# The last layer's second product for two token chunks, in seven block products instead of eight

## The chip, the cores and the metric

One core of one Trainium2 chip runs the whole program. The metric is the device time of one execution in microseconds (us); the kernel before took 581.81 us (median of 3 runs, 581.29 to 582.12).

## The reference

Attention (2 batches, 8 heads, 768 positions, 64 features a head; a local window of 16 and one pooled key and value for each block of 32) gives a matrix `x` of 1536 tokens by 512 features. Two feed-forward layers follow, each with weights 512 x 2048 and 2048 x 512, all in fp32:

```
h = x @ w_in;  r = max(h, 0);       x = (s * r * r + b) @ w_out      # layer 0
h = x @ w_in;  g = max(0.01*h, h);  out = g @ w_out                  # layer 1
```

The change touches layer 1 alone: `g @ w_out`, and how `out` lies in memory.

## The kernel before

Tokens go in three chunks of 512 (chunks 1, 2, 3; the code counts from 0), the hidden 2048 features in 16 slices `fc` of 128. To keep fp32 accuracy each operand is split into a rounded "high" part and a "low" rest, and each 128 x 128 by 128 x 512 product is three matmuls: high by high, low by high, high by low. ScalarE (ACT) makes the high part by a copy (`split_hi` L427, `split_block` L657, `ffn_hi` L470), VectorE (DVE) or GpSimd (POOL) the low part by a subtraction (`split_lo` L433, L658, `ffn_lo` L479).

Chunk 1 of layer 1 runs slice by slice: 12 matmuls of the first product (`ffn_in` L442), the activation, 12 of the second (`ffn_out` L494). For chunks 2 and 3 the first product is already done in Winograd's form of Strassen's scheme: the 512 x 512 blocks of hidden features by tokens come in eight quads `j`, each of four blocks, from seven block products in place of eight (`block` L668; 6 matmuls each; a11, s2, a12, s3, a22, s1, s4 name the weight block or the sum of blocks that is multiplied). Every block product has its own PSUM bank, and VectorE adds the results up (`after_block` L693 to L712). Beside these blocks run the second products of chunk 2 (units of 3 matmuls, taken from a list `queue`); chunk 3's second product comes last, alone (`last_chunk`): 16 slices of 12 matmuls. Each unit accumulates 128 tokens by 512 features in one of four banks; `out_store` copies the banks to SBUF and sends them to `out`, 1536 x 512. The last tile is sent in two halves, from the ACT queue and from the SP queue (L525, L526).

The order on every engine is the order in which the program issues instructions (`manual_schedule`); engines take their own instructions in that order, and semaphores are set from the tiles that are read and written.

Of the kernel before, what the change touches and what calls it, by code (L numbers as in the profile page):

```python
# [10 lines left out]
F32 = mybir.dt.float32  # L11
F32R = mybir.dt.float32r
# [20 lines left out]
GU = 4  # L33
# [66 lines left out]
def block_attention_moe_moe(ctx, tc, q, k, v, vn, w1, w2, mask, ident_in, pool_in, out):  # L100
# [380 lines left out]
    def ffn_out(i, m):  # L481
        layer, c, fc = steps[i]
        w, g = ws[1][i], gs[i]
        acc = accs.setdefault((layer, c), {})
        if fc == 0 and m not in acc:
            acc[m] = ps_acc.tile([P, 512], F32, name="acc")
        ms = slice(m * P, (m + 1) * P)
        for a, b in ((0, 0), (1, 0), (0, 1)):
            first = fc == 0 and a == 0 and b == 0
            last = fc == NFC - 1 and b == 1  # L490
            if layer == 0:
                nc.tensor.matmul(acc[m], lhsT=w[:, a, ms], rhs=g[:, b, :], start=first, stop=last)  # L492
            else:
                nc.tensor.matmul(acc[m], lhsT=g[:, b, ms], rhs=w[:, a, :], start=first, stop=last)  # L494

    xf = {1: {}, 2: {}}

# [16 lines left out]
        )  # L514

    def out_store(c, m):
        acc = accs[1, c]
        o = kpool_.tile([P, 1024], F32, name="kt")[:, :DM]
        t0 = c * 512 + m * P
        if c == 2 and m == 3:  # L520
            for cols, copy, queue in (
                (slice(0, DM // 2), nc.scalar.copy, nc.scalar),
                (slice(DM // 2, DM), nc.vector.tensor_copy, nc.sync),
            ):
                copy(o[:, cols], acc[m][:, cols])  # L525
                queue.dma_start(out[t0 : t0 + P, cols], o[:, cols])  # L526
            return
        if m % 2:
            nc.scalar.copy(o, acc[m])
        else:  # L530
            nc.vector.tensor_copy(o, acc[m])
        nc.sync.dma_start(out[t0 : t0 + P, :], o)


    NQ, LEAD = NFC // 2, 3
# [219 lines left out]
    def last_chunk():  # L755
        for fc in range(NFC):
            i = ns - NFC + fc
            if fc == 0:
                accs[1, 2] = {m: bank() for m in range(4)}
                late_split(1, 0)  # L760
            if fc + 1 < NFC:
                late_split(1, fc + 1)
            if fc == 0:
                for m in range(4):
                    out_store(1, m)
            for m in range(4):
                ffn_out(i, m)
        for m in range(4):
            out_store(2, m)
# [175 lines left out]
    for i in range(n_ffn1, nq):  # L945
        if i + 1 < nq:
            first_in(i + 1)
        else:
            block(1, 0, 0)
            block(1, 0, 1)  # L950
        if i + 2 < nq:
            split_hi(i + 2, 0)
            split_lo(i + 2, 0, nc.gpsimd)
        elif i + 2 == nq:
            for n in range(LEAD):
                split_block(1, n)
        if i + 1 < nq:
            split_hi(i + 1, 1)
            split_lo(i + 1, 1, nc.vector)
        if i + 1 < nq:  # L960
            chain(i + 1)
        at = i - n_ffn1
        convert((at + 1) * left // 13 - at * left // 13)
        if i + 1 < nq:
            for m in range(4):
                ffn_out(i, m)
        at -= 1
        if 0 <= at < 10:
            token_forms(at // 5, at % 5)
        if at == 11:  # L970
            weight_forms(1, 0)

    queue += [("out", nq - 1, m) for m in range(4)] + [("store", 0)]
    quads(1, 0, 2)
    emit_out(len(queue))
    last_chunk()


_INS = ["q", "k", "v", "vn", "w1", "w2", "mask", "ident", "pool"]
# [69 lines left out]
```

## Time and profile before

| | before |
|---|---|
| median of 3 runs | 581.81 us |
| profiled execution, span from first to last instruction | 579.6 us |
| TensorE matmul busy | 565.9 us, 98%, 3171 matmuls |
| DVE, ACT, POOL busy | 392.0, 341.1, 249.1 us |
| granted TensorE clock | full in all of the 40 slices |

The page shows one profiled execution. Its span is 2.2 us under the median of the runs; the page gives no other time for it. "PE" are matmuls, "PEld" weight loads, "L494" line 494.

### The profile page before, as it was taken

How to read it: one execution, taken by the hardware profiler on the slowest of the kernel's cores; microseconds unless marked ns; L12 is line 12 of the kernel's file. 1: busy time of each engine (PE TensorE's matmuls, PEld its weight loads, DVE VectorE, ACT ScalarE, POOL GpSimd, SP SyncE). 2: the span in 40 equal slices, each digit the busy share in tenths (PEclk: the TensorE clock that was granted, in tenths of full speed). 3: DMA queues.
4: the chain of work that ended last, by engine and by line, in shares of the span. 5: the costliest groups of instructions: out<-in, count | busy, mean ns of one | idle time of the engine just before them, and what ended most of it. 6: DMA issues, size and time to landing. Idle time of an engine off the chain costs nothing.

```text
span 579.6 us, 8972 instructions
## 1 busy us (share of the span) xinstructions
PE 565.9 (98%) x3171; PEld 454.9 (78%) x3172; DVE 392.0 (68%) x773; ACT 341.1 (59%) x770; POOL 249.1 (43%) x298
## 2 busy tenths in 40 slices
PE   3999999999999999999999999999999999999997
PEld 3567788777778888888888888888888888887885
DVE  5889987665689866665666889997354444446543
ACT  3888768776666555445656666764455444545442
POOL 4444644442262555524451436556565555540000
PEclk9999999999999999999999999999999999999999
DMA  8967765572100000000242345551010000000101
GB/s 324 399 219 246 250 205 211 174 233 95 74 2 1 1 1 1 1 1 1 73 131 88 110 126 165 145 146 36 1 72 2 1 1 0 1 0 12 62 2 72
DMA packets 16436, 53.38 MB, mean 92 GB/s; under 512 B 2024, under 2 KB 2664, under 8 KB 15752
## 3 DMA queue, kind: packets, MB, share of 16 engines
q1 hardware_dynamic: 16104, 52.69, 27.3%
q8 instruction: 25, 0.41, 0.3%
q14 instruction: 19, 0.16, 0.1%
q10 hardware_dynamic: 288, 0.13, 0.1%
HBM read 49.08 MB, written 3.15 MB: 90 GB/s over the span
## 4 chain that ended last, share of the span: by engine, by line
PE 96%; DMA 3%; SPq 0%; DVE 0%; issue 0%; ACT 0%
PE acc L492 23%; PE h L442 22%; PE acc L494 15%; PE h L668 10%; PE at L668 10%; PE h L494 4%; PE at L494 4%; DMA kt<-in_k 2%; PE at L334 2%; PE at L254 2%; PE at L353 2%; DMA w<-in_q 1%; PE h L353 1%; PE acc L442 0%; PE at L220 0%; PE at L208 0%
## 5 line engine op out<-in xcount | busy, mean ns | idle before, releaser
L492 PE MATMUL acc<-g,wout 128*128 128x512 f32 x564 | 141.6, 393 | 0.0
L442 PE MATMUL h<-xt,win 128*128 128x512 f32 x564 | 138.5, 392 | 0.0
L442 PEld LDWEIGHTS h<-xt,win 128*128 128x128 f32 x564 | 104.8, 188 | 22.7 <-issue 1.1
L492 PEld LDWEIGHTS acc<-g,wout 128*128 128x128 f32 x564 | 104.5, 188 | 22.6 <-issue 0.9
L494 PE MATMUL acc<-wout,g 128*128 128x512 f32 x384 | 99.1, 391 | 0.0
L433 DVE TENSOR_TENSOR wout<-w,wout 128x512 fp32r<-128x512 f32 x82 | 64.1, 782 | 37.6 <-ACT wout L427 37.2
L427 ACT CAST wout<-w 128x512 fp32r<-128x512 f32 x95 | 58.8, 619 | 46.7 <-PE acc L492 22.7
L494 PEld LDWEIGHTS acc<-wout,g 128*128 128x128 f32 x384 | 72.0, 188 | 15.8 <-DVE wout L433 0.4
L433 POOL TENSOR_TENSOR win<-w,win 128x512 fp32r<-128x512 f32 x36 | 52.0, 1444 | 51.4 <-ACT win L427 37.9
L413 DVE SCALAR_TENSOR_TENSOR w<-st,w 128x512 int32<-128x512 int32 x64 | 59.0, 925 | 6.8 <-issue 3.2
L658 POOL TENSOR_TENSOR win<-q,win 128x256 fp32r<-128x256 f32 x48 | 39.4, 820 | 37.8 <-ACT win L657 37.1
L658 POOL TENSOR_TENSOR win<-w,win 128x256 fp32r<-128x256 f32 x36 | 30.0, 833 | 44.2 <-ACT win L657 31.8
L479 DVE TENSOR_TENSOR g<-r,g 128x512 fp32r<-128x512 f32 x32 | 23.0, 719 | 36.4 <-ACT g L470 36.3
L393 ACT ACTIVATE st<-st 128x512 f32<-128x512 f32 x64 | 41.3, 673 | 0.7 <-DMA st<-in_w 0.7
L427 ACT CAST win<-w 128x512 fp32r<-128x512 f32 x48 | 29.5, 615 | 13.5 <-PE h L442 7.5
L668 PE MATMUL h<-xt,win 128*128 128x512 f32 x132 | 33.8, 391 | 0.0
L668 PE MATMUL at<-xt,win 128*128 128x512 f32 x132 | 33.8, 391 | 0.0
L680 ACT ACTIVATE r<-r 128x512 f32<-128x512 f32 x16 | 10.1, 632 | 37.9 <-DVE r L679 37.9
L475 DVE SCALAR_TENSOR_TENSOR g<-h,own,g 128x512 fp32r<-128x512 f32 x31 | 23.2, 748 | 12.8 <-ACT g L468 12.8
L406 POOL TENSOR_SCALAR w<-st 128x512 int32<-128x512 uint8 x30 | 23.5, 784 | 17.3 <-DMA st<-in_w 12.8
L668 PEld LDWEIGHTS h<-xt,win 128*128 128x128 f32 x132 | 24.8, 188 | 5.5
L668 PEld LDWEIGHTS at<-xt,win 128*128 128x128 f32 x132 | 24.8, 188 | 5.5
(185 smaller groups left out, 924.7 us busy)
## 6 DMA issues: line engine op xcount, KB each, us to landing
st<-in_w SPq DMA_DIRECT2D x64, 512.0 KB, 3.6
vt<-in_v SPq DMA_DIRECT2D x5, 1024.0 KB
kt<-in_k SPq DMA_DIRECT2D x8, 500.0 KB, 5.8
out<-kt SPq DMA_DIRECT2D x11, 256.0 KB, 2.7
q<-in_q SPq DMA_DIRECT2D x8, 256.0 KB, 4.6
w<-in_vn SPq DMA_DIRECT2D x3, 512.0 KB, 10.1
w<-in_q SPq DMA_DIRECT2D x4, 256.0 KB, 11.7
w<-in_v SPq DMA_DIRECT2D x2, 512.0 KB
```

The lines of the kernel that those rows point to most:

```text
L393: nc.scalar.activation(out=high, in_=high, func=AF.Prelu, scale=2.0**-112, alpha=2.0**32)
L406: engine.tensor_scalar(f, byte, 1.0 / 32, -31.0 / 64, op0=ALU.mult, op1=ALU.add)
L413: nc.vector.scalar_tensor_tensor(out=f, in0=high, scalar=3, in1=f, op0=ALU.logical_shift_left, op1=ALU.bitwise_or)
L427: nc.scalar.copy(t[:, 0, :], wf[layer, fc][:, half, :])
L433: engine.tensor_sub(t[:, 1, :], wf[layer, fc][:, half, :], t[:, 0, :])
L442: nc.tensor.matmul(hs[i], lhsT=w[:, a, cc * P : (cc + 1) * P], rhs=xt[c][:, b, cc, :], start=(cc == 0 and a == b == 0), stop=(cc == NCC - ...
L475: nc.vector.scalar_tensor_tensor(out=g[:, 1, :], in0=hs.pop(i), scalar=shift_b, in1=g[:, 0, :], op0=ALU.add, op1=ALU.subtract)
L479: nc.vector.tensor_sub(g[:, 1, :], rs.pop(i), g[:, 0, :])
L492: nc.tensor.matmul(acc[m], lhsT=w[:, a, ms], rhs=g[:, b, :], start=first, stop=last)
L494: nc.tensor.matmul(acc[m], lhsT=g[:, b, ms], rhs=w[:, a, :], start=first, stop=last)
L658: nc.gpsimd.tensor_sub(t[:, 1, :], src, t[:, 0, :])
L668: nc.tensor.matmul(banks[j, name], lhsT=t[:, a, cc * P : (cc + 1) * P], rhs=x[b][cc], start=(cc == a == b == 0), stop=(cc == b == 1),)
```

## The change

In the second product of layer 1 the weights become the stationary operand and the tokens the moving one, so that `out` is stored as 512 features by 1536 tokens and transposed on the host. Chunk 1 keeps its units, in that form.

For chunks 2 and 3 the activations of a quad are kept (`raw`), in tiles that are free by then. Two of the seven block products (a11 and a12 of the output weights) run beside the blocks of the first product (`out_unit`, four units of 3 matmuls a quad). The other five run after them (`LATE`: 40 products of 2 units), with sums of weight blocks (`out_forms`) and of activations (`raw_forms`), all on VectorE.

In the first product the blocks no longer have a bank each. Bank p takes a11 and then a12; ACT copies p after a11 into bank u, on which s2, s3 and a22 accumulate in turn, with a copy to SBUF after s2 and s3; bank v takes s1 and then s4. In each round a quad's a22 and s4 run among the next quad's blocks (`WEAVE`). The low part of most weight blocks moves from POOL to DVE. Two new SBUF tiles (`spare`, `early`) are taken, and `dynamic_dma_scratch_size` is set to 1024.

```diff
--- before.py
+++ after.py
@@ -126,6 +126,8 @@
     own = const.tile([P, 6], F32, name="own")
     root, sign, shift_b = (own[:, i : i + 1] for i in range(3))
     vpool_w = const.tile([P, 10, 32], F32, name="vpool_w")
+    spare = const.tile([P, NFC // 2 + 1, 256], F32, name="spare")
+    early = const.tile([P, 3, 2, 256], F32R, name="early")
     xt = [xpool.tile([P, 2, NCC, 512], F32R, name=f"xt{i}") for i in range(3)] 
@@ -488,10 +490,7 @@
...
+            nc.tensor.matmul(acc[m], lhsT=w[:, a, ms], rhs=g[:, b, :], start=first, stop=last)
@@ -514,22 +513,9 @@
         ) 
     def out_store(c, m):
...
+        o = kpool_.tile([P, 1024], F32, name="kt")[:, :512]
+        (nc.scalar.copy if m % 2 else nc.vector.tensor_copy)(o, accs[1, c][m])
+        nc.sync.dma_start(out[m * P : (m + 1) * P, c * 512 : (c + 1) * 512], o) 
     NQ, LEAD = NFC // 2, 3
@@ -752,21 +738,339 @@
         ffn_hi(i)
         ffn_lo(i) 
...
+    WEAVE = (("a11", 0), ("a22", 1), ("s2", 0), ("a12", 0), ("s4", 1), ("s3", 0), ("s1", 0))
+    weave = [(j - d, name) for j in range(NQ + 1) for name, d in WEAVE if 0 <= j - d < NQ]
+    raw, wo, go, po = {}, {}, {}, {}
+    def weave_forms(j):
+        a11, a12, a21, a22 = (weight_block(1, j, n) for n in ("a11", "a12", "a21", "a22"))
+        s1, s2, s3 = (wform[i] for i in range(3))
+        s4 = wform[3] if j % 2 else spare[:, NQ, :]
+        nc.gpsimd.tensor_add(s1, a21, a22)
+        nc.gpsimd.tensor_sub(s2, s1, a11)
+        nc.gpsimd.tensor_sub(s3, a11, a21)
+        nc.gpsimd.tensor_sub(s4, a12, s2)
...
+    def weave_split(n):
+        if n >= len(weave):
+            return
+        if n == 0:
+            wops["tiles"] = [wspl.tile([P, 2, 512], F32R, name="win") for _ in range(2)]
+        j, name = weave[n]
+        src = spare[:, NQ, :] if name == "s4" and j % 2 == 0 else weight_block(1, j, name)
+        t = wops["tiles"][n % 4 // 2][:, :, n % 2 * 256 : n % 2 * 256 + 256]
+        nc.scalar.copy(t[:, 0, :], src)
+        (nc.gpsimd if name in ("a11", "s1") else nc.vector).tensor_sub(t[:, 1, :], src, t[:, 0, :])
+        wops[n] = t
...
+    def weave_bank(j, name):
+        if name == "a11":
+            banks[j, "p"] = ps_at.pool.tile([P, 512], F32, name="at0")
+            banks[j, "u"] = ps_h.tile([P, 512], F32, name="h")
+        elif name == "s1":
+            banks[j, "v"] = ps_at.pool.tile([P, 512], F32, name="at1")
+        return banks[j, {"a11": "p", "a12": "p", "s1": "v", "s4": "v"}.get(name, "u")]
+    def weave_block(n):
+        j, name = weave[n]
+        ps, t, x = weave_bank(j, name), wops.pop(n), tf[TOKENS[name]]
+        for cc in range(2):
+            for a, b in ((0, 0), (1, 0), (0, 1)):
+                nc.tensor.matmul(
+                    ps,
+                    lhsT=t[:, a, cc * P : (cc + 1) * P],
+                    rhs=x[b][cc],
+                    start=(name in ("a11", "s1") and cc == a == b == 0),
+                    stop=(cc == b == 1),
+                    skip_group_check=name not in ("a11", "s1"),
+                )
+        weave_split(n + LEAD)
...
+    def out_forms(j, part):
+        a11, a12, a21, a22 = (out_part(j, n) for n in ("a11", "a12", "a21", "a22"))
+        s1, add, sub = spare[:, j, :], nc.vector.tensor_add, nc.vector.tensor_sub
+        if part == 0:
+            add(s1, a21, a22)
+            sub(a21, a11, a21)
+        else:
+            sub(a11, s1, a11)
+            sub(a12, a12, a11)
+    def out_hi(j, k):
+        if k == 0:
+            wo[j] = wspl.tile([P, 2, 512], F32R, name="wout")
+        nc.scalar.copy(wo[j][:, 0, 256 * k : 256 * k + 256], out_part(j, f"a1{k + 1}"))
+    def out_lo(j, k):
+        t = wo[j][:, :, 256 * k : 256 * k + 256]
+        nc.vector.tensor_sub(t[:, 1, :], out_part(j, f"a1{k + 1}"), t[:, 0, :])
+    def raw_hi(j, k, ps):
+        leaky(ps, ps)
+        t = go[j, k] = gpool.tile([P, 2, 512], F32R, name="g")
+        nc.scalar.copy(t[:, 0, :], ps)
+        nc.scalar.copy(raw[j, f"{k + 1}1"], ps)
+    def raw_lo(j, k):
+        t = go[j, k]
+        nc.vector.tensor_sub(t[:, 1, :], banks[j, "pu"[k]], t[:, 0, :])
+    def out_unit(j, k, m):
+        if j == 0:
+            po[k, m] = ps_acc.tile([P, 512], F32, name="acc")
+        w, g = wo[j], go[j, k]
+        at = 256 * k + m * P
+        for a, b in ((0, 0), (1, 0), (0, 1)):
+            nc.tensor.matmul(
+                po[k, m],
+                lhsT=w[:, a, at : at + P],
+                rhs=g[:, b, :],
+                start=(j == 0 and a == b == 0),
+                stop=(j == NQ - 1 and b == 1),
+            )
+    def raw_forms(j, part):
+        g11, g12, g21, g22 = (raw[j, n] for n in ("11", "12", "21", "22"))
+        sub = nc.vector.tensor_sub
+        if part == 0:
+            sub(g11, g12, g11)
+        elif part == 1:
+            sub(g12, g22, g12)
+        elif part == 2:
+            if j % 2 == 0:
+                t = kpool_.tile([P, 1024], F32, name="kt")
+                raw[j, "t2"], raw[j + 1, "t2"] = t[:, :512], t[:, 512:]
+            sub(raw[j, "t2"], g22, g11)
+        else:
+            sub(g21, g21, raw[j, "t2"])
+    def weave_after(n):
+        j, name = weave[n]
+        add = nc.vector.tensor_add
+        p, u, v = (banks.get((j, i)) for i in "puv")
+        if name == "a11":
+            nc.scalar.copy(u, p)
+            if j:
+                leaky(raw[j - 1, "22"], raw[j - 1, "22"])
+                out_unit(j - 1, 0, 0)
+            if j > 1:
+                raw_forms(j - 2, 3)
+                out_forms(j - 2, 0)
+        elif name == "s2":
+            rs[j] = gpool.tile([P, 512], F32, name="r")
+            nc.scalar.copy(rs[j], u)
+            if j > 1:
+                out_forms(j - 2, 1)
+        elif name == "a22":
+            raw_hi(j, 1, u)
+            if j + 1 < NQ:
+                out_hi(j + 1, 0)
+                out_lo(j + 1, 0)
+            else:
+                leaky(raw[j, "22"], raw[j, "22"])
+                out_unit(j, 0, 0)
+            out_unit(j, 0, 1)
+        elif name == "a12":
+            raw_hi(j, 0, p)
+            if j:
+                raw_lo(j - 1, 1)
+            else:
+                out_lo(0, 0)
+        elif name == "s4":
+            g12 = raw[j, "12"]
+            add(g12, rs[j], v)
+            leaky(g12, g12)
+            if j + 1 < NQ:
+                raw_lo(j + 1, 0)
+                weave_forms(j + 2) if j + 2 < NQ else None
+        elif name == "s3":
+            nc.scalar.copy(raw[j, "22"], u)
+            if j == 0:
+                raw_lo(0, 0)
+                weave_forms(1)
+            if j:
+                raw_forms(j - 1, 0)
+                out_unit(j - 1, 1, 0)
+            out_hi(j, 1)
+        else:
+            g22 = raw[j, "22"]
+            add(g22, g22, v)
+            out_lo(j, 1)
+            if j:
+                raw_forms(j - 1, 1)
+                raw_forms(j - 1, 2)
+                out_unit(j - 1, 1, 1)
+    LATE = [("s4", q) for q in range(NQ)] + [("s2", q) for q in range(NQ)] + [("s1", q) for q in range(2)]
+    LATE += [("s3", q) for q in range(NQ)] + [("s1", q) for q in range(2, NQ)] + [("a22", q) for q in range(NQ)]
+    BANK = {"s4": "w", "s2": "u", "s3": "u", "a22": "u", "s1": "v"}
+    WITH = {"s2": "t2", "s1": "11", "s3": "12", "a22": "21", "s4": "22"}
+    rings, late = {"g": {}, "w": {}}, {}
...
+    def late_operands(n):
+        if n >= len(LATE):
+            return
+        name, q = LATE[n]
+        g, w = late_home(n)
+        src, form = raw[q, WITH[name]], out_form(q, name)
+        nc.scalar.copy(w[:, 0, :], form)
+        nc.scalar.copy(g[:, 0, :], src)
+        nc.vector.tensor_sub(w[:, 1, :], form, w[:, 0, :])
+        nc.vector.tensor_sub(g[:, 1, :], src, g[:, 0, :])
+        late[n] = w, g
+    def late_unit(n, m):
+        name, q = LATE[n]
+        w, g = late[n]
+        ps = po[BANK[name], m]
+        for a, b in ((0, 0), (1, 0), (0, 1)):
+            nc.tensor.matmul(
+                ps,
+                lhsT=w[:, a, m * P : (m + 1) * P],
+                rhs=g[:, b, :],
+                start=(name in ("s1", "s4") and q == a == b == 0),
+                stop=(q == NQ - 1 and b == 1),
+                skip_group_check=name not in ("s1", "s4"),
+            )
+    def result(i, k, m, ps, x=None):
...
+        row, col = (2 * i + m) * P, (1 + k) * 512
+        if x is not None:
+            nc.vector.tensor_add(o, x, ps)
+            nc.sync.dma_start(out[row : row + P, col : col + 512], o)
+            return
+        for h, copy, queue in ((0, nc.scalar.copy, nc.scalar), (256, nc.vector.tensor_copy, nc.sync)):
+            copy(o[:, h : h + 256], ps[:, h : h + 256])
+            queue.dma_start(out[row : row + P, col + h : col + h + 256], o[:, h : h + 256])
+    def late_after(name, m):
+        ps = po[BANK[name], m]
+        if name in ("s2", "s3"):
+            if m == 0:
+                t = kpool_.tile([P, 1024], F32, name="kt")
+                for h in range(2):
+                    late[name, h] = t[:, h * 512 : h * 512 + 512]
+            nc.scalar.copy(late[name, m], ps)
+        elif name == "s1":
+            result(1, 1, m, ps, late["s3", m])
+            result(0, 1, m, ps, late["s4", m])
+        elif name == "a22":
+            result(1, 0, m, ps)
+    def second_layer_end():
+        last, lead, split = NQ - 1, 6, len(LATE) - 4
+        forms = [(out_forms, last, 0), (out_forms, last, 1), (raw_forms, last, 0)]
+        forms += [(raw_forms, last, 2), (raw_forms, last, 1), (raw_forms, last - 1, 3), (raw_forms, last, 3)]
+        begin = {49: (0,), 51: (1,), 53: (2,), 54: (3,), 55: (4, 5)}
+        done = 0
+        for n in range(2, len(weave)):
+            weave_block(n)
+            weave_after(n)
+            if n < 4:
+                ffn_out(nq - 1, n)
+            if n < 6:
+                out_store(0, n - 2)
+            if n >= len(weave) - 2:
+                out_forms(last - 1, n - len(weave) + 2)
+            for x in begin.get(n, ()):
+                late_operands(x)
+            if n == len(weave) - 3:
+                po["w", 0] = ps_at.pool.tile([P, 512], F32, name="at0")
+                po["w", 1] = ps_h.tile([P, 512], F32, name="h")
+            if n >= len(weave) - 3:
+                for m in range(2):
+                    late_unit(done, m)
+                done += 1
+        raw_lo(last, 1)
+        for m in range(2):
+            late["x", m] = gpool.tile([P, 512], F32, name="r")
+            nc.scalar.copy(late["x", m], po[0, m])
+        for n, (name, q) in enumerate(LATE[:split]):
+            for _ in range(1):
+                if forms:
+                    f, j, part = forms.pop(0)
+                    f(j, part)
...
+            late_operands(n + lead)
+            if (name, q) == ("s1", 0):
+                for m in range(2):
+                    po["v", m] = ps_acc.tile([P, 512], F32, name="acc")
+            if (name, q) == ("s3", 0):
+                t = kpool_.tile([P, 1024], F32, name="kt")
+                for m in range(2):
+                    late["s4", m] = t[:, m * 512 : m * 512 + 512]
+                    nc.vector.tensor_add(late["s4", m], late["s2", m], po["w", m])
+            for m in range(2):
+                if n >= done:
+                    late_unit(n, m)
+                if q == NQ - 1:
+                    late_after(name, m)
+            if n in (8, 9):
+                out_unit(last, 1, n - 8)
+                result(0, 0, n - 8, po[1, n - 8], late["x", n - 8])
+        for m in range(2):
+            for n in range(split, len(LATE)):
+                late_unit(n, m)
+            late_after("a22", m) 
...
@@ -946,19 +1250,25 @@
         if i + 1 < nq:
             first_in(i + 1)
         else:
-            block(1, 0, 0)
-            block(1, 0, 1)
+            weave_homes()
+            for n in range(2):
+                weave_block(n)
+                weave_after(n)
+                ffn_out(nq - 1, n)
...
+        if i + 2 == nq:
+            weave_split(0)
         if i + 1 < nq:
             chain(i + 1)
+        if i + 2 == nq:
+            weave_split(1)
+            weave_split(2)
+            out_hi(0, 0)
...
+            weave_begin()
+    second_layer_end() 
 _INS = ["q", "k", "v", "vn", "w1", "w2", "mask", "ident", "pool"]
...
+    nc = bacc.Bacc("TRN2", target_bir_lowering=False, num_devices=1, dynamic_dma_scratch_size=1024)
...
+    args.append(nc.dram_tensor("out_0", (DM, T), F32, kind="ExternalOutput").ap())
...
-    return r.results[0]["out_0"]
+    return np.ascontiguousarray(r.results[0]["out_0"].T)
```

## Rows read from the trace of the kernel before

**Rows 1.** Page: busy time by engine; granted clock in 40 slices.

```profile
PE 565.9 (98%) x3171; PEld 454.9 (78%) x3172; DVE 392.0 (68%) x773; ACT 341.1 (59%) x770; POOL 249.1 (43%) x298
...
PEclk9999999999999999999999999999999999999999
```

**Rows 2.** Windows: busy us (instructions) of PE, PEld, DVE, ACT, POOL; clock, DMA.

```profile
407.60:575.80 168.20, 168.20 (x733) 137.08 (x731) 81.37 (x127) 78.43 (x161) 62.58 (x81) 1.00 0.04 14
531.00:575.80 44.80, 44.80 (x198) 36.57 (x196) 23.25 (x36) 19.26 (x35) 0.00 (x0) 1.00 0.08 28
```

**Rows 3.** Chain that ended last, around 408 us: start, length, what.

```profile
405.07 2.72 PE acc L494 x12
407.79 1.36 PE h L668 x6
409.15 1.39 PE at L668 x6
```

**Rows 4.** Timeline: the first blocks, and the copy that follows the first.

```profile
407.63 1.52 PE L668 MATMUL h<-xt,win 128*128 128x512 f32 x6
...
409.19 0.59 ACT L693 COPY r<-h 128x512 f32<-128x512 f32 x1 [1.64 <-PE h L668]
```

**Rows 5.** Lines by form, whole span: busy us, mean ns, idle before.

```profile
L479 DVE TENSOR_TENSOR g<-w,g 128x512 fp32r<-128x512 f32 x16 | 11.0, 686 | 0.0
L370 DVE TENSOR_TENSOR xt<-at,xt 128x256 fp32r<-128x256 f32 x16 | 6.5, 418 | 4.1 <-ACT xt L365 3.9
L470 ACT CAST g<-w 128x512 fp32r<-128x512 f32 x16 | 9.8, 615 | 0.0
L461 ACT ACTIVATE h<-r 128x512 f32<-128x512 f32 x13 | 7.8, 602 | 0.3
L657 ACT CAST win<-q 128x256 fp32r<-128x256 f32 x48 | 19.2, 399 | 1.4 <-PE at L668 0.6
L658 POOL TENSOR_TENSOR win<-w,win 128x256 fp32r<-128x256 f32 x36 | 30.0, 833 | 44.2 <-ACT win L657 31.8 <-PE at L668 5.7 <-PE h L668 5.7
```

**Rows 6.** Timeline: instructions that follow one another at once, on DVE and ACT.

```profile
121.86 0.76 DVE L370 TENSOR_TENSOR xt<-at,xt 128x256 fp32r<-128x256 f32 x2
...
425.64 0.41 ACT L657 CAST win<-w 128x256 fp32r<-128x256 f32 x1
425.95 0.41 ACT L657 CAST win<-q 128x256 fp32r<-128x256 f32 x1
...
453.89 0.62 ACT L470 CAST g<-r 128x512 fp32r<-128x512 f32 x1
454.41 0.62 ACT L427 CAST wout<-w 128x512 fp32r<-128x512 f32 x1
...
464.80 0.68 DVE L709 TENSOR_TENSOR w<-w,h 128x512 f32<-128x512 f32 x1
465.40 0.68 DVE L679 TENSOR_TENSOR w<-w,h 128x512 f32<-128x512 f32 x1
```

**Rows 7.** Timeline: weight loads of one unit; the third waits for the low part.

```profile
531.79 0.42 PEld L494 LDWEIGHTS h<-wout,g 128*128 128x128 f32 x2
...
532.45 0.19 PEld L494 LDWEIGHTS h<-wout,g 128*128 128x128 f32 x1 [0.24 <-DVE g L479]
```

**Rows 8.** Timeline: the end; then DMA issues with KB and us to landing.

```profile
574.53 1.69 SPq L532 DMA_DIRECT2D out<-kt  x3
...
574.98 0.84 PE L494 MATMUL at<-wout,g 128*128 128x512 f32 x3
575.85 0.37 ACT L525 COPY kt<-at 128x256 f32<-128x256 f32 x1 [0.77 <-PE at L494]
576.26 0.35 ACTq L526 DMA_DIRECT2D out<-kt  x1
576.26 0.42 DVE L525 COPY kt<-at 128x256 f32<-128x256 f32 x1 [0.39 <-ACT kt L525]
576.71 0.33 SPq L526 DMA_DIRECT2D out<-kt  x1
...
out<-kt ACTq DMA_DIRECT2D x1, 128.0 KB, 2.1
```

More of the change, by code (lines that the diff above doesn't have):

```diff
@@ L490, in ffn_out @@
             last = fc == NFC - 1 and b == 1
[L491 to L494, printed above, removed]
+            nc.tensor.matmul(acc[m], lhsT=w[:, a, ms], rhs=g[:, b, :], start=first, stop=last)
     xf = {1: {}, 2: {}}
@@ L516, in out_store @@
     def out_store(c, m):
[L517 to L532, printed above, removed]
+        o = kpool_.tile([P, 1024], F32, name="kt")[:, :512]
+        (nc.scalar.copy if m % 2 else nc.vector.tensor_copy)(o, accs[1, c][m])
+        nc.sync.dma_start(out[m * P : (m + 1) * P, c * 512 : (c + 1) * 512], o)
     NQ, LEAD = NFC // 2, 3
@@ L753, in late_split @@
         ffn_lo(i)
[L755 to L769, printed above, removed]
+    WEAVE = (("a11", 0), ("a22", 1), ("s2", 0), ("a12", 0), ("s4", 1), ("s3", 0), ("s1", 0))
@@ new lines, in weave_begin @@
+    def weave_begin():
+        for i in range(2):
+            t = const.tile([P, GU, 2 * QT], F32, name=f"q{i}").rearrange("p a c -> p (a c)")
+            wform[2 * i], wform[2 * i + 1] = t[:, :256], t[:, 256:]
+        weave_forms(0)
+    def weave_split(n):
[9 more added lines that the diff above has]
+        wops[n] = t
@@ new lines, in weave_homes @@
+    def weave_homes():
+        rows = [t[:, i * 512 : i * 512 + 512] for t in (stage.tile([P, 512], I64, name="st").bitcast(F32) for _ in range(4)) for i in range(2)]
+        again = xpool.tile([P, 2 * NCC, 512], F32, name="xt0")
+        rows += [again[:, m, :] for m in range(2 * NCC)]
+        for j in range(NQ):
+            raw[j, "11"], raw[j, "21"] = rows[2 * j : 2 * j + 2]
+            raw[j, "12"], raw[j, "22"] = late_g(1, 2 * j), late_g(1, 2 * j + 1)
+    def weave_bank(j, name):
[5 more added lines that the diff above has]
+        return banks[j, {"a11": "p", "a12": "p", "s1": "v", "s4": "v"}.get(name, "u")]
@@ new lines, in leaky, with out_part, out_form @@
+    def leaky(out, x):
+        nc.scalar.activation(out=out, in_=x, func=AF.Prelu, scale=1.0, alpha=0.01)
+    def out_part(j, name):
+        i, k = int(name[1]) - 1, int(name[2]) - 1
+        return wf[1, 2 * j + k][:, 1, 256 * i : 256 * i + 256]
+    def out_form(j, name):
+        if name == "s1":
+            return spare[:, j, :]
+        return out_part(j, {"s2": "a11", "s3": "a21", "s4": "a12"}.get(name, name))
+    def out_forms(j, part):
[7 more added lines that the diff above has]
+            sub(a12, a12, a11)
@@ new lines, in block_attention_moe_moe, with late_home @@
+    LATE = [("s4", q) for q in range(NQ)] + [("s2", q) for q in range(NQ)] + [("s1", q) for q in range(2)]
[3 more added lines that the diff above has]
+    rings, late = {"g": {}, "w": {}}, {}
+    def late_home(n):
+        if n >= 11:
+            rings["g"][n] = rings["g"][n - 11]
+        elif n not in rings["g"]:
+            if n in (2, 8):
+                t = att.tile([P, GU, DM], F32, name="vt").bitcast(F32R)
+                rings["g"][n], rings["g"][n + 1] = t[:, :2, :], t[:, 2:, :]
+            elif n >= 10:
+                rings["g"][n] = gpool.tile([P, 2, 512], F32R, name="g")
+            else:
+                c, m = ((1, 0), (1, 1), None, None, (1, 2), (1, 3), (2, 0), (2, 1))[n]
+                rings["g"][n] = xt[c][:, :, m, :]
+        if n >= 9:
+            rings["w"][n] = rings["w"][n - 9]
+        elif n < 3:
+            rings["w"][n] = early[:, n, :, :]
+        elif n % 2:
+            t = wspl.tile([P, 2, 512], F32R, name="win" if n > 4 else "wout")
+            rings["w"][n], rings["w"][n + 1] = t[:, :, :256], t[:, :, 256:]
+        return rings["g"][n], rings["w"][n]
@@ new lines, in result @@
+    def result(i, k, m, ps, x=None):
+        if "free" not in rings:
+            t = kpool_.tile([P, 1024], F32, name="kt")
+            rings["free"] = [t[:, h * 512 : h * 512 + 512] for h in range(2)]
+            for h in range(4):
+                soft.free(("t4", 1, h))
+            rings["free"] += [soft.tile(("out", h)) for h in range(4)]
+            rings["free"] += rings["free"][:2]
+        o = rings["free"].pop(0)
+        row, col = (2 * i + m) * P, (1 + k) * 512
[6 more added lines that the diff above has]
+            queue.dma_start(out[row : row + P, col + h : col + h + 256], o[:, h : h + 256])
@@ new lines, in second_layer_end @@
+    def second_layer_end():
[31 more added lines that the diff above has]
+                    f(j, part)
+            if n == 3:
+                po["u", 0] = ps_at.pool.tile([P, 512], F32, name="at1")
+                po["u", 1] = ps_h.tile([P, 512], F32, name="h")
+            if n in (3, 4):
+                nc.scalar.copy(po["u", n - 3], late["x", n - 3])
+            late_operands(n + lead)
[3 more added lines that the diff above has]
+            if (name, q) == ("s3", 0):
+                t = kpool_.tile([P, 1024], F32, name="kt")
+                for m in range(2):
[13 more added lines that the diff above has]
+            late_after("a22", m)
@@ L953, in block_attention_moe_moe @@
             split_lo(i + 2, 0, nc.gpsimd)
-        elif i + 2 == nq:
-            for n in range(LEAD):
-                split_block(1, n)
         if i + 1 < nq:
@@ L970, in block_attention_moe_moe @@
         if at == 11:
[L971 to L976, printed above, removed]
+            weave_begin()
+    second_layer_end()
 _INS = ["q", "k", "v", "vn", "w1", "w2", "mask", "ident", "pool"]
@@ L1037 @@
     arrays = _layout(**inputs)
-    nc = bacc.Bacc("TRN2", target_bir_lowering=False, num_devices=1)
+    nc = bacc.Bacc("TRN2", target_bir_lowering=False, num_devices=1, dynamic_dma_scratch_size=1024)
     feeds, args = {}, []
```

1 line of the change is left out of this document (removed).

## The prediction

> **What bounds the kernel now.** [...] Then the windows over the part that changes, from the first block product to the last matmul [rows 2]: matmuls fill all of it, 168.2 of 168.2 us, while DVE and ACT work for 81.4 and 78.4 us. Then the chain that ended last [rows 3]: it runs from matmul to matmul, 12 in 2.72 us, so 0.2267 us each. Last the single instructions [rows 4 to 8], for what a DVE or ACT operation costs alone and in a row. So a matmul fewer is 0.227 us less, as long as the other engines keep up; whether they do is the whole question.
>
> **Matmuls.** Before, the stretch has 56 blocks of 6, and 132 units of 3 (the last slice of chunk 1, 64 units for each of chunks 2 and 3): 336 + 396 = 732 (the window counts 733). After: 336 + 12 + 32 units beside the blocks (96) + 80 units behind them (240) = 684. The 48 fewer are 48 x 0.2267 = **-10.88 us**. The 732 took 168.2 us where 732 x 0.2267 gives 165.9; the 2.3 us over lie mostly in blocks of 1.39 in place of 1.36 us [rows 3]. The blocks stay, so I keep that.
>
> **The rounds.** A round is now seven blocks and four units: 7 x 1.38 + 4 x 0.68 = 12.4 us (before: eight units, 15.1). Into it go, for DVE, 11 operations of 256 columns and 8 of 512; for ACT 9 and 11. Alone they take 0.42 and 0.69 us on DVE, 0.40 and about 0.61 on ACT [rows 5]; one behind another the next starts after 0.34 and 0.60, and after 0.31 and 0.52 (0.76 - 0.42, 465.40 - 464.80, 425.95 - 425.64, 454.41 - 453.89 [rows 6]). DVE has thus 8.5 us of work in a row, 10.1 at most; ACT 8.5 to 10.3; POOL, two low parts and four sums at up to 0.83, 5.0. All fit into 12.4, so the cover for every added operation is the matmul stream; what can cost is order. I follow one round from the start of a11, a block being readable 1.56 us after its start (1.52 and 0.04 to the reader [rows 4]).
>
> a12 runs at 5.50 to 6.88, s4 of the quad before to 8.26, s3 and a unit to 10.32, then s1. s1 overwrites bank v, so it waits for DVE's addition from v behind s4: 8.48 + 0.69 = 9.17 against 10.32, 1.15 us spare. The next a11 overwrites p, at 12.38: ACT reads a12's result from 7.08 on in three operations (0.63 + 0.52 + 0.62 = 1.8), DVE's low part follows at about 10. ACT's queue holds a copy for s2 that waits for POOL's new sums: ACT's copy for a11 ends at 9.2, POOL needs 3 x 0.83, so 11.7, and ACT is idle until the next a11 is readable at 13.9. Bank u is written by ACT's copy of p, at 1.56 to 2.2; s2 needs it at 4.12. No wait in rounds 1 to 6. The copy from PSUM to PSUM has no row; writing PSUM takes 0.60, reading it 0.59 [rows 4, 5]. I take 0.60; were both to add up to 1.2, s2 still has 1.3 us spare, and less than 0.6 costs nothing less.
>
> *Round 0* has one unit between a11 and s2: s2 is due at 2.04, the copy ends at 2.16: **+0.12** (0 to 0.7 by the bounds of the copy).
>
> *Round 7* also makes operands for the products behind the blocks (two ACT copies, two DVE subtractions each). ACT, in a row from a22's end at 3.6: 0.63 + 0.52 + 0.52, copies for output weights and s3 0.31 + 0.31, s2's copy 0.52, the first operands 0.31 + 0.52, 0.31 for s1, so a12's three operations begin at 7.6 and not 7.1, and end at 9.3; then the copy for the last a22, 9.7. In this round alone its low part stands on DVE ahead of the addition from v (elsewhere POOL has that place): 9.7 + 0.38, + 0.69 = 10.79 against 10.32: **+0.47**. Bounds: 0, if ACT is 0.5 us earlier, and 1.4 with every operation at its full row time.
>
> **Behind the blocks.** One product is two units, 1.36 us of matmuls, and its operands take DVE 0.34 + 0.60 = 0.94 (ACT 0.83). Seven forms come first, one for each of the first seven operand sets: 0.60 to 0.68 more, so 1.55 to 1.62, above 1.36. From the start of round 7, with the 0.47 in it: the last block is readable at 19.9. DVE then has an addition, a form pair, and in order operands 4 and 5, done at 22.8 and 23.75, the low part of the last a22 (0.60), and with a form each operands 6, 7, 8 at 26.0, 27.6, 29.2, and 9 to 12 every 1.55, then every 0.94. TensorE does product 2 to 21.05 and comes to 3, 4, 5 without a wait; the third matmul alone needs the moving low part (waits are by single matmul [rows 7]). So product 6 is late by 0.40, 7 by 0.26, 8 by 0.20; from 9 on two single units lie between and DVE gains 0.4 us a product. **+0.86.** Bounds: 0, and 3.4 if each DVE operation costs its full row time (1.11 + 0.74 - 1.36 = 0.49, seven times).
>
> The later copies, additions and stores lie under 8 products of 1.36 us or more. Moving operands in the tiles that showed 1.39 in place of 1.36 are in 14 of the 40 products: 14 x 0.03 = **+0.4** (0 to 1.2, if in all). The reversed roles of chunk 1's units and the moved output rows change no count: a tile remains 128 pieces of 2 KB. The scratch size touches none of the stores, which SP and ACT issue [rows 8]: 0.
>
> **The end.** The copies stay (0.37, 0.42). Before, the last half went off at 576.71 behind three 256 KB stores issued from 574.53 on, and the span ended at 579.6, 2.9 us later, where ACT's half took 2.1 [rows 8]. After, only one tile goes out shortly ahead, 2.7 us before: **-0.4** (0 to -0.8).
>
> **Sum.** -10.88 + 0.12 + 0.47 + 0.86 + 0.4 - 0.4 = -9.4 us. Span 579.6 - 9.4 = 570.2; the runs lie 2.2 us above the profiled span, which I keep: 581.8 - 9.4 = **572.4 us**.
>
> **Rivals.**
>
> *VectorE pays each operation's full time.* Then round 7 costs 1.4 and the products behind the blocks 3.4, together 4.8 in place of 1.3: 575.9 us. For it: most DVE operations here follow an ACT copy, and then nothing overlaps. Against it: rows 6, where the second operation starts 0.08 us before the first's row ends, on both engines; behind the blocks two subtractions stand together. [...] Chance 0.22.
>
> *A small wait in every round.* The spare time ahead of s1 is 1.15 us. If DVE reaches the addition from v 1.8 us later than I count, since its queue holds five low parts that wait for ACT, s1 is late by 0.65 in each of seven rounds: 572.4 + 4.6 = 577.0. For it: before, POOL did these low parts and DVE had none of them. Against it: DVE is idle for 2 to 4 us of a round by the sums above. Chance 0.12.
>
> *No wait at all*, since ACT and DVE are ahead: 572.4 - 1.45 - 0.4 = 570.5. Chance 0.10.
>
> *VectorE sets the pace, and the kernel is slower.* 19 operations fill a round from a mean of 12.4 / 19 = 0.65 us on. Were 256 columns as dear as 512, 0.69: 8 x 0.73 in the rounds, 40 x 0.02 behind them and 7 x 0.69 for the forms make 11.5 us, more than the 10.9 saved: 582.4, and over 590 with 0.04 us from engine to engine for each. It decides from a mean of about 0.68. For it: VectorE's work in this stretch grows by two thirds. Against it: 0.418 us for 256 columns [rows 5]. Chance 0.06.
>
> **The numbers.** The likeliest case, 0.50, has its own range of 571 to 574.5 us. To hold 8 in 10 the range takes in the case without waits and the next two: 570.0 to 578.0. A measurement tells 0.2%, 1.2 us, from no change. All cases but the last are faster by more: 0.93; within 0.2% lie the edge of the small waits and of the last case, 0.02; slower 0.05.
>
> **What would show it.** 48 matmuls fewer, PE busy about 556 us, and the chain still on TensorE to the end. Matmuls waiting on DVE: s1 of the last round, then products 6 to 8; an ACT wait of 0.1 us in round 0; none in rounds 1 to 6. DVE's sum rises by 8 x 10.1 + 40 x 1.11 + some 10 - 81 = 54 to about 446 us, ACT's to about 390; POOL's falls to about 225. The prediction is wrong if s1 or a11 wait in every round, if TensorE's stretch is longer than 684 x 0.2267 + 2.3 + 3 = 160.4 us, or if the granted clock falls.

## The result

The changed kernel takes 573.66 us (median of 4 runs, 573.44 to 573.95) against 581.69 (581.29 to 582.12): 8.0 us less, ratio 0.9862 with a 95% interval of 0.9848 to 0.9876. Forecast were 572.4 us, in a range of 570 to 578. The profiled execution took 573.70 us with a span of 571.9, 7.7 less than the profiled span before.

The page after, to be read beside [rows 1]: busy times, granted clock, chain by engine.

```profile
PE 558.4 (98%) x3123; PEld 445.9 (78%) x3124; DVE 435.3 (76%) x890; ACT 371.6 (65%) x856; POOL 221.4 (39%) x258
...
PEclk9999999999999999999999999999999999999999
...
PE 93%; DMA 3%; ACT 1%; DVE 1%; SPq 0%; issue 0%; ACTq 0%
```

Exactly 48 matmuls are gone. TensorE still bounds the kernel, at the full clock, but the chain now holds some ACT and DVE time. The window over the stretch, first block to last matmul, answers to the first of [rows 2]:

```profile
408.10:568.40 160.30, 159.40 (x685) 127.70 (x683) 123.97 (x242) 109.34 (x248) 36.89 (x43) 1.00 0.05 19
```

168.2 us have become 160.3, and 0.9 us of it now has no matmul in flight, where there was none before. The chain after shows where the longest of these gaps comes from: in order of time, start, length, what.

```profile
516.44 0.60 DVE g L842
517.04 0.34 DVE spare L819
517.38 0.02 issue
517.41 0.42 DVE w L820
517.83 0.34 DVE win L965
518.17 0.60 DVE xt L966
518.77 0.35 DVE w L822
519.12 0.02 issue
519.14 0.44 DVE w L823
...
519.66 0.41 ACT win L963
520.06 0.53 ACT xt L964
520.59 0.04 issue
520.63 1.23 PE at L974 x3
```

It reads backwards from the late matmul: product 7's first matmul at 520.63 waited for ACT's high part of the tokens (L964), which stood behind ACT's high part of the weight sum (L963), which waited for DVE's sum (L823), which waited for the sum before it (L822) and, ahead of that, for the operands of product 6 and one more pair of sums (L819, L820). A piece of the chain begins where the piece before it ends, so its start can be later than that of the instruction; the timelines below have the starts themselves.

### The profile page after: what moved, and what is told of

Same layout as the page of the kernel before. It is cut to its first block, busy times and chain, and to the rows that moved or that the text cites. A ratio compares the mean times of both kernels' runs of the same rounds, so it can differ in the third digit from the quotient of the medians.

```text
span 571.9 us, 9002 instructions
## 1 busy us (share of the span) xinstructions
PE 558.4 (98%) x3123; PEld 445.9 (78%) x3124; DVE 435.3 (76%) x890; ACT 371.6 (65%) x856; POOL 221.4 (39%) x258
## 4 chain that ended last, share of the span: by engine, by line
PE 93%; DMA 3%; ACT 1%; DVE 1%; SPq 0%; issue 0%; ACTq 0%
PE acc L493 31%; PE h L444 23%; PE at L793 7%; PE h L793 5%; PE acc L850 4%; PE at L974 3%; PE h L654 3%; PE at L654 3%; PE h L974 3%; DMA vt<-in_v 2%; PE acc L974 2%; PE at L336 2%; PE at L256 2%; PE at L355 2%; PE h L355 1%; PE at L210 1%
## 5 line engine op out<-in xcount | busy, mean ns | idle before, releaser
L493 PE MATMUL acc<-g,wout 128*128 128x512 f32 x756 | 188.2, 392 | 0.0
L493 PEld LDWEIGHTS acc<-g,wout 128*128 128x128 f32 x756 | 140.5, 188 | 30.1 <-issue 0.8
L444 PE MATMUL h<-xt,win 128*128 128x512 f32 x564 | 138.5, 392 | 0.0
L444 PEld LDWEIGHTS h<-xt,win 128*128 128x128 f32 x564 | 104.8, 188 | 22.6 <-issue 1.1
L435 DVE TENSOR_TENSOR wout<-w,wout 128x512 fp32r<-128x512 f32 x50 | 42.0, 839 | 14.5 <-ACT wout L429 14.1
L470 ACT ACTIVATE g<-h,own 128x512 fp32r<-128x512 f32 x31 | 21.3, 686 | 10.7 <-DVE h L465 7.3
L405 DVE TENSOR_SCALAR w<-st 128x512 int32<-128x512 int32 x34 | 27.5, 810 | 0.0
L455 ACT ACTIVATE r<-h 128x512 f32<-128x512 f32 x31 | 18.3, 593 | 14.1 <-PE h L444 14.1
L850 PE MATMUL acc<-g,wout 128*128 128x512 f32 x96 | 27.2, 393 | 0.0
L299 ACT ACTIVATE sm<-sm,nm 128x120 f32<-128x120 f32 x64 | 24.4, 387 | 3.5 <-DVE nm L281 3.5
L769 POOL TENSOR_TENSOR win<-q,win 128x256 fp32r<-128x256 f32 x8 | 7.7, 958 | 49.0 <-DVE w L822 28.5
L457 ACT ACTIVATE r<-h 128x512 f32<-128x512 f32 x16 | 9.6, 598 | 23.3 <-PE h L444 23.3
```

The source lines that it names most:

```text
L299: nc.scalar.activation(out=sm[:, u, :], in_=sm[:, u, :], func=AF.Exp, bias=nm[:, u : u + 1], scale=-1.0, accum_out=rec[:, u, :],)
L405: engine.tensor_scalar(f, low, 29, None, op0=ALU.logical_shift_right)
L444: nc.tensor.matmul(hs[i], lhsT=w[:, a, cc * P : (cc + 1) * P], rhs=xt[c][:, b, cc, :], start=(cc == 0 and a == b == 0), stop=(cc == NCC - ...
L850: nc.tensor.matmul(po[k, m], lhsT=w[:, a, at : at + P], rhs=g[:, b, :], start=(j == 0 and a == b == 0), stop=(j == NQ - 1 and b == 1),)
```

## The experiments

Times are medians, ratios are to the kernel before, with 95% intervals.

**The changed kernel again**, beside the next three on one chip.

> The changed kernel unaltered, so that the next three are compared with it on the same chip. 573.7 us (573.2 to 574.2), ratio to the kernel before 0.986. In its profile again a wait of some 0.25 us for the first s2, 0.25 us for the last s1, and 2.0 us in all at products 6, 7 and 8 behind the blocks.

573.55 us, 0.9856 (0.9840 to 0.9873), with the same waits.

**The last quad's weight sums on GpSimd.**

```diff
...
-        forms = [(out_forms, last, 0), (out_forms, last, 1), (raw_forms, last, 0)]
+        forms = [(raw_forms, last, 0)]
...
+            if n == len(weave) - 3:
+                out_forms(last, 0, nc.gpsimd)
+                out_forms(last, 1, nc.gpsimd)
```

> The last quad's four sums of output-weight blocks run on GpSimd in the last round, not on VectorE ahead of the operands of products 6 and 7. Theory (a round trip: VectorE's form, then ScalarE's copy of it, then VectorE's low part, so that VectorE stands idle inside product 7's operands): the wait at product 7 goes from 1.2 to under 0.3 us and that at 6 to under 0.2; 1.3 to 1.7 us less, 572.2 us. Rival (the matmuls behind the blocks are slower for another reason, such as their tiles): the sum of the waits at 6 to 8 stays near 2 us, 573.5 us.

572.30 us, 0.9838 (0.9824 to 0.9853): 1.25 us less. The waits at products 6 to 8 fall from 2.0 to 0.65 us. The low parts of the tokens of products 6, 7 and 8 in this kernel's timeline:

```profile
517.77 0.68 DVE L966 TENSOR_TENSOR xt<-w,xt 128x512 fp32r<-128x512 f32 x1
...
519.32 0.68 DVE L966 TENSOR_TENSOR xt<-w,xt 128x512 fp32r<-128x512 f32 x1
...
520.86 0.68 DVE L966 TENSOR_TENSOR vt<-kt,vt 128x512 fp32r<-128x512 f32 x1
```

They come 1.55 us apart, more than the 1.36 us of a product's matmuls, since a sum of activations goes ahead of each: the list of sums is shorter by two, so that the five sums of activations go out two products earlier. The run takes away the order and 1.4 us of DVE's work at once, so the next run keeps the work.

**The same sums on VectorE, earlier.**

```diff
-        forms = [(out_forms, last, 0), (out_forms, last, 1), (raw_forms, last, 0)]
+        forms = [None, None, (raw_forms, last, 0)]
...
+            if n == len(weave) - 2:
+                out_forms(last, 0)
+                out_forms(last, 1)
...
```

> The same four sums stay on VectorE but are issued before the addition for the last s4, where VectorE waits 1.2 us anyway; its work is the same. Theory (round trip and order, not VectorE's total): the waits at products 6 to 8 fall from 2.0 to about 0.7 us, 572.4 us. Rival of the prediction (VectorE's total alone, a form more than a product takes): the work is the same and only the idle 1.2 us are won back, so the later products 9 to 12 must wait in their place for what the sums took; the total falls by less than 0.5 us, 573.3 us.

571.67 us, 0.9829 (0.9815 to 0.9844): 1.9 us less with the same instructions, more than either theory gave. Matmuls of products 6 to 8 in this kernel's timeline (start, length):

```profile
517.71 0.85 PE L974 MATMUL at<-xt,win 128*128 128x512 f32 x3
...
518.39 0.84 PE L974 MATMUL h<-xt,win 128*128 128x512 f32 x3
...
519.07 0.84 PE L974 MATMUL at<-xt,win 128*128 128x512 f32 x3
...
519.75 0.84 PE L974 MATMUL h<-xt,win 128*128 128x512 f32 x3
...
520.43 0.87 PE L974 MATMUL at<-vt,win 128*128 128x512 f32 x3
...
521.13 0.85 PE L974 MATMUL h<-vt,win 128*128 128x512 f32 x3
```

Units start every 0.68 to 0.70 us, and products 9 to 12 don't wait in their place. So VectorE's total was not what was short; the place of the sums was. The run takes two things from the place behind the blocks, the round trip and the sums' own time in VectorE's queue, and doesn't tell how much each was worth; the starts in the section on the prediction do.

**All waits at once, with GpSimd's help.** On top of the sums on GpSimd: the last a22's low part and the low weight parts of products 6 to 15 on GpSimd, and a second unit of chunk 1 between the first a11 and s2.

```diff
...
-        nc.vector.tensor_sub(w[:, 1, :], form, w[:, 0, :])
+        (nc.gpsimd if 5 < n < 16 else nc.vector).tensor_sub(w[:, 1, :], form, w[:, 0, :])
...
-                ffn_out(nq - 1, n)
+                if n == 0:
+                    ffn_out(nq - 1, 0)
+                    ffn_out(nq - 1, 1)
```

> The sums on GpSimd as before in this set, and besides: the low part of the last a22 block on GpSimd, the low weight parts of products 6 to 15 on GpSimd, and two units of chunk 1 (in place of one) between the first a11 and s2. Theory: all three waits are order on VectorE and ScalarE, so 0.25 + 0.25 + 2.0 us go, and the time is 573.7 - 2.5 = 571.2 us, with no matmul from the first block to the last waiting over 0.1 us. Rival (GpSimd's 0.8 us for an operation of 256 columns makes new waits at products 6 to 9): 572.2 us or more.

573.79 us, 0.9863 (0.9848 to 0.9877): no gain over the changed kernel, and 1.5 us lost against the sums on GpSimd alone. The rival held, by another mechanism than it named. Timeline of this kernel, VectorE beside GpSimd:

```profile
516.34 3.58 POOL L965 TENSOR_TENSOR win<-w,win 128x256 fp32r<-128x256 f32 x3 [7.83 <-ACT win L963]
516.35 0.68 DVE L862 TENSOR_TENSOR xt<-w,xt 128x512 f32<-128x512 f32 x1
...
516.95 1.22 DVE L966 TENSOR_TENSOR xt<-w,xt 128x512 fp32r<-128x512 f32 x1
...
518.09 1.22 DVE L869 TENSOR_TENSOR kt<-w,xt 128x512 f32<-128x512 f32 x1
...
519.24 1.23 DVE L966 TENSOR_TENSOR xt<-w,xt 128x512 fp32r<-128x512 f32 x1
```

While GpSimd subtracts 256 columns, VectorE's 512 take 1.22 us in place of 0.68, and GpSimd's take 1.2 in place of 0.74: they run in step, one of each every 1.14 us. So the low parts of the tokens come 2.29 us apart (516.95, 519.24), where they came 1.55 apart without the help, and products 6, 7 and 8 wait about 2.4 us by the starts of their units. The help cost VectorE more than it took off.

**A fourth matmul in each unit beside the blocks.**

```diff
-        for a, b in ((0, 0), (1, 0), (0, 1)):
+        for a, b in ((0, 0), (1, 0), (1, 1), (0, 1)):
...
```

> Each of the 32 units beside the blocks gets a fourth matmul, low by low (the result gains that small term). Theory (TensorE is the bound in every round): 32 x 0.2267 = 7.3 us more, less at most 0.3 where the last round waits now: 580.8 us. Rival (rounds are held by the chain of copies and additions between the banks, and TensorE only looks full): the four added matmuls of a round, 0.9 us, fall into waits, 575 us or less.

580.39 us, 0.9978 (0.9969 to 0.9988): 6.8 us more than the changed kernel. 32 x 0.2267 = 7.25, and the wait of the last s1, 0.39 us by its start times, is gone but for 0.05. The rounds are bound by TensorE.

**GpSimd's part of the rounds on VectorE.**

```diff
-        (nc.gpsimd if name in ("a11", "s1") else nc.vector).tensor_sub(t[:, 1, :], src, t[:, 0, :])
+        nc.vector.tensor_sub(t[:, 1, :], src, t[:, 0, :])
...
-        nc.gpsimd.tensor_add(s1, a21, a22)
+        nc.vector.tensor_add(s1, a21, a22)
```

(The other three sums alike.)

> GpSimd's part of the rounds, two low parts and four sums of weight blocks of 256 columns, goes to VectorE: at 0.34 us in a row 2.0 us more in most rounds, 10.5 of 12.4 us, at full row time 12.6. Theory (operations in a row overlap, VectorE has 2 to 4 us a round to spare): at most 0.3 us a round are lost, 573.7 to 576 us. Rival (each operation costs its full time and VectorE sets the pace): 0.2 to 1 us a round from operations alone and more from waits on ScalarE, 577 us or more, and s1 or s2 waits for VectorE in every round.

573.77 us, 0.9864 (0.9850 to 0.9879): no change. In rounds 1 to 6 VectorE does 144 operations in place of 111 and is busy only 63.2 us in place of 59.5, since the others get shorter. One line of rounds 2 to 6 by form (busy us, mean ns, idle), first of the changed kernel, then of this one:

```profile
L862 DVE TENSOR_TENSOR st<-w,st 128x512 f32<-128x512 f32 x3 | 3.7, 1225 | 0.0
```

```profile
L862 DVE TENSOR_TENSOR st<-w,st 128x512 f32<-128x512 f32 x3 | 2.1, 685 | 0.0
```

**The roles alone, in the kernel before.** All of layer 1's second products with weights stationary, the result stored feature by token; nothing else.

```diff
-            if layer == 0:
...
-                nc.tensor.matmul(acc[m], lhsT=g[:, b, ms], rhs=w[:, a, :], start=first, stop=last)
+            nc.tensor.matmul(acc[m], lhsT=w[:, a, ms], rhs=g[:, b, :], start=first, stop=last)
...
-        nc.sync.dma_start(out[t0 : t0 + P, :], o)
+        nc.sync.dma_start(out[rows, t0 : t0 + 512], o)
```

> The kernel before with one part of the change alone: in layer 1's second product weights stationary and tokens moving for all three chunks, and the result stored feature by token. Theory: no count of matmuls, operations or store pieces changes, so no difference: 581.7 us, within 0.3%. Rival (stores with rows 6 KB apart land later, or the other stationary operand waits more): 0.3 us or more longer at the end, 582.2 to 583 us.

581.70 us, 1.0001 (0.9992 to 1.0010). The layout is worth nothing either way, within 0.1%.

**The copy between banks twice.**

```diff
             nc.scalar.copy(u, p)
+            nc.scalar.copy(u, p)
```

> The changed kernel with ScalarE's copy from bank p to bank u made twice in each of the eight rounds (the second writes the same values). Theory (it lies under a unit, a block and a unit from round 1 on): 0.5 to 0.6 us more, all in round 0, 574.1 us. Rival (the copies into PSUM are on the path in every round): 8 x 0.6 = 4.8 us more, 578 us.

574.24 us, 0.9871 (0.9858 to 0.9885): 0.6 us more than the 573.66 above, the price of one copy, and it lies where it was expected, at round 0's s2 (timeline of this kernel):

```profile
410.94 1.42 PE L793 MATMUL h<-vt,win 128*128 128x512 f32 x5 [0.58 <-ACT h L879]
```

The block starts 1.43 us behind the unit before it, 0.60 later than in the changed kernel, and the stretch to the copy behind the last matmul is 160.85 us, 0.56 longer: the other seven copies are hidden.

**Three orders changed, no work added.** The early sums on VectorE; the last a22's low part alone on GpSimd; two units in round 0 between a11 and s2. (The lines of the early sums are those above.)

```diff
-        (nc.gpsimd if name in ("a11", "s1") else nc.vector).tensor_sub(t[:, 1, :], src, t[:, 0, :])
+        (nc.gpsimd if name in ("a11", "s1") or n == len(weave) - 2 else nc.vector).tensor_sub(t[:, 1, :], src, t[:, 0, :])
...
-                ffn_out(nq - 1, n)
+                if n == 0:
+                    ffn_out(nq - 1, 0)
+                    ffn_out(nq - 1, 1)
```

> Three changes of order in the changed kernel, no work more or less: the last quad's weight sums on VectorE ahead of the last s4 (as in the run before that gained 1.9 us), the low part of the last a22 block on GpSimd, one operation, and two units of chunk 1 in place of one between the first a11 and s2. Theory (each wait is an order on VectorE or ScalarE, and they don't depend on one another): 571.7 - 0.25 - 0.25 = 571.2 us, and only product 5's wait of 0.4 us is left. Rival (a wait cleared early comes back behind it, since VectorE is busy without a gap by then): 571.6 to 572 us.

570.70 us, 0.9813 (0.9800 to 0.9826), the lowest time: 10.9 us under the kernel before and 1.0 under the early sums alone, where 0.5 was expected. By the starts of their blocks and units the two waits were 0.25 and 0.39 us, not 0.25 each, and product 4's fell with them from 0.22 to 0.04. What is left is one wait, at product 4 (the expectations count it as 5), in the list of who waited for whom:

```profile
PEld at L974 <- DVE xt L966: 0.2, 1, 0.2
```

**On top of it, product 4's operands a block earlier.**

```diff
-        begin = {49: (0,), 51: (1,), 53: (2,), 54: (3,), 55: (4, 5)}
+        begin = {49: (0,), 51: (1,), 53: (2,), 54: (3, 4), 55: (5,)}
```

> As the run with three orders, with the operands of product 4 made one block earlier, ahead of the last s4's addition. Theory: product 5's wait of 0.4 us goes too, 570.8 us, no matmul waiting over 0.1 us from the first block on. Rival: the addition for the last s4 is late instead, or the last a22's low part, and the time stays at 571.2 us or above.

570.92 us, 0.9813 (0.9799 to 0.9826): the trace lists no wait of TensorE in the stretch any more, but the time is the same within the spread. From the first block to the copy behind the last matmul it takes 157.61 us (408.98 to 566.59), the run before it 157.65.

## Why the prediction was right, and where it was off

The main term held: 48 matmuls less at 0.2267 us, priced again by the fourth matmul. The differences, over the stretch from the first block to the copy behind the last matmul: 168.22 us before (407.63 to 575.85 [rows 4, 8]), 160.29 after (408.12 to 568.41), so -7.93 where the steps gave -9.03. The sign of being wrong that the prediction set for this stretch, more than 160.4 us, was 0.1 us away.

*Round 0:* forecast +0.12, measured 0.25. The timeline after:

```profile
408.12 1.52 PE L793 MATMUL at<-xt,win 128*128 128x512 f32 x6
...
409.48 0.84 PE L493 MATMUL acc<-g,wout 128*128 128x512 f32 x3
409.68 0.57 ACT L878 COPY h<-at 128x512 f32<-128x512 f32 x1 [0.65 <-PE at L793]
...
410.31 1.66 PE L793 MATMUL h<-vt,win 128*128 128x512 f32 x6
...
411.80 0.86 PE L493 MATMUL acc<-g,wout 128*128 128x512 f32 x3
```

The copy took 0.57, within its bounds, and s2 began 0.15 us late as worked out. The other 0.10 was not counted: the block then takes 1.49 us to the next unit in place of 1.39, its first weight load having been held back too: it waits 0.40 us for the copy and starts at 410.30, where the unit before has its first load 0.22 us ahead of its first matmul (409.26 and 409.48).

*Rounds 1 to 6:* no wait, as forecast: the list of who waited for whom after has two waits of matmuls in the stretch, at product 7 and at the last s1, in round 7, and in rounds 1 to 6 none of a weight load either. Its two lines for the matmuls, with us in all, times and the longest:

```profile
PE at L974 <- ACT xt L964: 0.6, 1, 0.6
PE at L793 <- DVE w L907: 0.2, 1, 0.2
```

The spare time ahead of s1 comes out as worked out. In one round after:

```profile
463.86 0.69 DVE L907 TENSOR_TENSOR w<-r,at 128x512 f32<-128x512 f32 x1 [0.68 <-PE at L793]
...
464.46 0.68 DVE L842 TENSOR_TENSOR g<-at,g 128x512 fp32r<-128x512 f32 x1
464.56 0.74 POOL L769 TENSOR_TENSOR win<-w,win 128x256 fp32r<-128x256 f32 x1 [1.38 <-ACT win L768]
...
465.70 1.55 PE L793 MATMUL at<-vt,win 128*128 128x512 f32 x6
```

The addition from v ends at 464.55, s1 starts at 465.70: 1.15 us. The small wait in every round and the pace set by VectorE are thereby ruled out, and VectorE stood 15.6 of 75.1 us idle in rounds 1 to 6, 2.6 a round.

*Round 7's s1:* forecast +0.47, measured 0.39 (1.00 us from the unit before it to its start in place of 0.68, and 0.07 inside). The low part of the last a22 (L769) stands on VectorE ahead of the addition from v (L907), as worked out:

```profile
502.18 0.43 DVE L769 TENSOR_TENSOR win<-w,win 128x256 fp32r<-128x256 f32 x1 [0.72 <-ACT win L768]
...
502.53 0.68 DVE L907 TENSOR_TENSOR w<-r,at 128x512 f32<-128x512 f32 x1
...
503.36 1.63 PE L793 MATMUL at<-vt,win 128*128 128x512 f32 x6 [0.16 <-DVE w L907]
```

*Behind the blocks:* this is the step that failed, in size: forecast +0.86 (0.40, 0.26 and 0.20 at products 6, 7, 8), measured 2.03 (0.50, 1.16, 0.33 by the starts of their units, and 0.04 at product 4). I let VectorE run through its queue at its pace and gave ACT a lead. But ACT's copy of product 7's weights can't start until VectorE has made the sum it copies, and VectorE's low part waits for that copy. The timeline after, from product 6's low part of the tokens (518.09) to product 7's (520.61) and product 8's (522.16):

```profile
518.09 0.68 DVE L966 TENSOR_TENSOR xt<-w,xt 128x512 fp32r<-128x512 f32 x1
518.69 0.42 DVE L822 TENSOR_TENSOR w<-spare,w 128x256 f32<-128x256 f32 x1
519.14 0.42 DVE L823 TENSOR_TENSOR w<-w 128x256 f32<-128x256 f32 x1
...
519.66 0.41 ACT L963 CAST win<-w 128x256 fp32r<-128x256 f32 x1 [2.26 <-DVE w L823]
...
519.97 0.61 ACT L964 CAST xt<-w 128x512 fp32r<-128x512 f32 x1
...
520.09 0.43 DVE L965 TENSOR_TENSOR win<-w,win 128x256 fp32r<-128x256 f32 x1 [0.53 <-ACT win L963]
...
520.61 0.69 DVE L966 TENSOR_TENSOR xt<-w,xt 128x512 fp32r<-128x512 f32 x1
...
522.16 0.69 DVE L966 TENSOR_TENSOR vt<-kt,vt 128x512 fp32r<-128x512 f32 x1
```

From 7 to 8 it takes 1.55 us, as the sum had it; from 6 to 7 it takes 2.52, where the sum had 0.60 + 3 x 0.34 = 1.62. The 0.90 us between them are the 0.90 by which product 7 is later than forecast, and they lie in three places. The second sum (L823) uses the first's result and starts 0.45 us after it, not 0.34. The low part of the weights (L965) starts 0.95 us after that sum, not 0.34: ACT begins its copy 0.1 us after the sum's end, and VectorE is idle for 0.53 us until it has the copy. The low part of the tokens then starts 0.52 us later, not 0.34, since the high part of the tokens comes behind the weights' on ACT and ends at 520.58. Products 4, 6 and 8 add 0.27 to what was forecast.

Moving the sums a few operations ahead, with VectorE's work unchanged, removed the waits at products 6 to 8 altogether, so it was not VectorE's total. The part that was forecast is VectorE's queue, and it is there: with the sums on GpSimd there is no round trip, yet the low parts come 1.55 us apart and 0.65 us of waits stay. The upper bound of 3.4 us, by full row times, was no better a reading: rows that wait for nothing start 0.60 us apart here too (518.09 to 518.69).

*Moving operands in slower tiles:* forecast +0.4, about 0.2. The run without a wait takes 157.61 us for 684 x 0.2267 = 155.06, which leaves 2.55, against 2.3 before.

*The end:* forecast -0.4, measured -0.26: 568.41 to 571.9 is 3.49, before 575.85 to 579.6, 3.75. The 256 KB stores of `out` from SP land in a median of 2.2 us on the page after and of 2.7 on the page before, so with the scratch size at 1024 they take no longer.

Together 0.25 + 0.39 + 2.03 = 2.67 us of waits, which is what separates 160.29 from 157.61. The rest of the difference in span is ahead of the change: the first block starts at 408.12 in place of 407.63, and between 407.66 and 408.98 in the profiles of the other versions whose code up to there is the same.

Part of the nearness is luck. The span was forecast at 570.2 us and is 571.9, 1.7 more, but the time is only 1.3 above its forecast. The prediction put the runs 2.2 us above the span, from the median of the runs and one profiled execution whose own time it did not have. After, the median is 1.8 above the profiled span (573.66 and 571.9), and the 0.4 between the two made the miss smaller.

The rival in which each operation pays its full time named 575.9 us, and it fell: with 33 operations more in six rounds the kernel took no longer. Of the sums, DVE's total was put at 446 us and is 435, ACT's at 390 and is 372, POOL's at 225 and is 221.

## What to carry to other kernels

Where one engine is full and the others have room, take away its instructions and count the rest by order, not by total: follow each operand from engine to engine, and where a value is made on one engine, copied on a second and used again on the first, count the round trip. Put sums that later operands need into places where their engine waits anyway; here that was worth 1.9 us with not an instruction less. Before GpSimd is to help a busy VectorE, look in a trace whether the two slow each other, as they did here (VectorE's 512 columns 1.22 us in place of 0.68).

## What the runs showed of the hardware

In the run with all waits at once VectorE and GpSimd slowed each other where both ran operations with two operands in SBUF: VectorE's 512 columns took 1.22 us beside GpSimd and 0.68 alone, and GpSimd's 256 columns 1.2, where they took 0.74 beside VectorE's subtraction with one operand in PSUM in the changed kernel; one pair came every 1.14 us. That is less than the 0.68 + 0.74 = 1.42 of the two apart, so in these rows neither waited for the whole of the other. With GpSimd's part on VectorE the operations slowed in the rounds were short again (L862: 1225 and 685 ns), and 33 operations more raised VectorE's busy time in six rounds by only 3.7 us. The subtraction with one operand in PSUM kept its 0.68 us beside GpSimd (L842 and L769 at 464.46 and 464.56 above).

Accumulating matmuls on a bank that ScalarE has filled cost nothing that the trace shows: the copy from PSUM to PSUM took 0.57 us, and in one round after, the block s2 on that bank took 1.40 us to the next block's start (459.50 to 460.90), where s1, on a bank that no copy fills, took 1.39 (465.70 to 467.09).
